# Gated linear and softmax attention on one core: first x chunk transposed on TensorE, value projection by head group, three-bank slots everywhere, new durations in the layout model

## The chip, the cores and the metric

The kernel runs on one core of a Trainium2 chip. The metric is the device time of one execution in microseconds (us), lower is better. Before the change it is 1020.41 us (median of three runs, 1017.95 to 1022.5). TensorE is called PE below, its weight loads PEld, VectorE DVE, ScalarE ACT, GpSimd POOL, and the engine that issues most transfers SP. "The clock" is the granted TensorE clock that the profile shows, as a share of full speed.

## The reference

`x` is 2048 x 512 in bf16, with 32 heads of 16 columns. Branch A is a linear attention with softmax features, branch B an ordinary softmax attention, and a gate mixes them by row.

```python
def _A_ref(x, wqkv, w_phi, wo):
    ...                                            # q, k, v = split(x @ wqkv)
    pq = jnp.einsum("bhsd,hdf->bhsf", q, w_phi)    # the same for k
    phi_q = jnp.concatenate([_softmax(pq), _softmax(-pq)], axis=-1)
    ...
    kv = jnp.einsum("bhsf,bhsd->bhfd", phi_k, v)
    z = jnp.einsum("bhsf->bhf", phi_k)
    num = jnp.einsum("bhqf,bhfd->bhqd", phi_q, kv)
    den = jnp.einsum("bhqf,bhf->bhq", phi_q, z)[..., None] + 1e-6
    return (num / den) ... @ wo

def _B_ref(x, wqkv, wo):
    ...                                            # q, k, v = split(x @ wqkv)
    scores = jnp.einsum("bhqd,bhkd->bhqk", q, k) * (Dh ** -0.5)
    return einsum(softmax(scores), v) ... @ wo

g = _sigmoid((x * gate_w).sum(-1, keepdims=True))
return g * a + (1 - g) * b
```

The heavy part is branch B: 32 heads of 2048 x 2048 scores are 134 million exponentials, and ACT computes every one of them.

## The kernel before

The scores are cut into 2048 tiles of 128 keys x 512 queries. A *slot* is a few tiles next to each other in PSUM: PE computes their scores (QK), ACT takes the exponential of the whole slot in one instruction, PE multiplies with V (PV) and accumulates. Two slots alternate, so ACT can run on one while PE fills the other. A *fill* is any other work for PE (projections, the whole of branch A, the outputs) that is squeezed in between and drained by DVE.

The order of instructions on each engine is not written down. Every operation is registered with an engine, a guessed duration and a priority, and a list scheduler, the *layout model*, plays the program through with those guesses and fixes the order. Each engine is then given its list in that order, with semaphores between the engines. A wrong guess therefore never gives a wrong result, but it can put an instruction in a place where it blocks its engine.

```python
MARGIN = 0.35                       # model: extra delay from DVE/POOL to PE/ACT, and after a DMA
...
op.end = t + op.dur + op.lat        # the scheduler knows nothing but these numbers
...
bS = [Bank(f"S{i}", psS[:, 512 * i:512 * (i + 1)]) for i in range(6)]   # six banks of slots
EARLY = [bM, bS[2], bS[5], bO]      # banks that early fills may use
MISC = [bM, bS[2], bS[5]]           # banks that other fills may use
...
for c in range(QC):                 # x arrives transposed by DMA, 4 chunks of 512 rows
    for t in range(KT):
        dma("sp", 0.01 * (4 * c + t), lambda e, c=c, t=t: e.dma_start_transpose(
            xT[:, t, NQ * c:NQ * (c + 1)], A_x[0, NQ * c:NQ * (c + 1), 128 * t:128 * (t + 1)]),
            [("xT", t, c)], name=f"x{c}_{t}", issue=0.95, lat=2.2)
for i, (nm, o) in enumerate((("wbk", D), ("wbq", 0), ("wbv", 2 * D))):   # 512 KB each
    dma("act", 0.001 * i, lambda e, o=o: e.dma_start(W_B[:, :, o:o + D], wb_v[:, :, o:o + D]),
        [nm], name=nm, lat=3.0 + 1.5 * i)
...
MM = 0.216                          # model: one fill matmul of 512 columns
...
def v_fill(st, prio, banks=None):   # V of 128 tokens for all 32 heads: 4 matmuls of 512 columns
    f, mm = fill(prio, proj([xT[:, t, 128 * st:128 * (st + 1)] for t in range(KT)],
                            [W_B[:, t, 2 * D:3 * D] for t in range(KT)]), ...)
...
n = 2 if s < 64 else min(3, NTILE - s)   # slots: two tiles wide in the first 64 tiles, then three
...
def add_qk(j):
    def fn(e):
        for m, s in enumerate(range(s0, s0 + n)):
            ins = e.matmul(psS[:, 512 * (base + m):512 * (base + m + 1)],
                           lhsT=kT_B[32 * i:32 * i + 32, hg // 2, 128 * kt:128 * (kt + 1)],
                           rhs=qz[32 * i:32 * i + 32, qc % 2, hg, :], ...)
    op = P.add("pe", 0.30, -100, fn, ...)
...
# branch A, normalising one group: PE multiplies phi(q) with kv|z into psM, DVE divides
f, mm = fill(prio + 0.1, mms, [("phiQT", b), "kz0", "kz1"], ..., dur=0.065)
drain(f, mm, "dve", 0.15, -3, ... e.tensor_single_scalar(dr3, ap[...], 1e-6, ALU.add), last=False)
P.add("dve", 0.12, -3, lambda e, dr=dr: e.reciprocal(dr, dr), ...)
P.add("dve", 0.1, -3, lambda e, dr=dr: e.tensor_scalar(dr, dr, g128[:, i:i + 1], None, op0=ALU.mult), ...)
drain(f, mm, "dve", 0.42, -3, fn, ...)       # oA = num * dr, frees psM
```

Because slots are only two tiles wide in the first 64 tiles, banks 2 and 5 of the slots are free for fills there: the first block needs all of V, and that is 16 fills.

The softmax here doesn't subtract the row's maximum and nothing guards it: scores larger than these inputs give would overflow.

Of the kernel before, what the change touches and what calls it, by code (L numbers as in the profile page):

```python
# [6 lines left out]
BF16 = mybir.dt.bfloat16  # L7
# [6 lines left out]
D = 512  # L14
# [12 lines left out]
MARGIN = 0.35  # L27
# [233 lines left out]
def _build(ctx, nc, A_x, A_wqkv, A_w_phi, A_wo, B_wqkv, B_wo, gate_w, out):  # L261
# [34 lines left out]
    fin = sb([128, 2, D], name="fin")  # L296
# [10 lines left out]
    gwb = sb([128, KT, 128], name="gwb")  # L307
# [11 lines left out]
    for b in (0, 1, 3, 4):  # L319
        bS[b].free = False  # L320
    EARLY = [bM, bS[2], bS[5], bO]
    MISC = [bM, bS[2], bS[5]]
# [7 lines left out]
    for c in range(QC):  # L330
        for t in range(KT):
            dma("sp", 0.01 * (4 * c + t), lambda e, c=c, t=t: e.dma_start_transpose(
                xT[:, t, NQ * c:NQ * (c + 1)], A_x[0, NQ * c:NQ * (c + 1), 128 * t:128 * (t + 1)]),
                [("xT", t, c)], name=f"x{c}_{t}", issue=0.95, lat=2.2)
    wb_v = B_wqkv.rearrange("(t p) c -> p t c", p=128)
    wa_v = A_wqkv.rearrange("(t p) c -> p t c", p=128)
    for i, (nm, o) in enumerate((("wbk", D), ("wbq", 0), ("wbv", 2 * D))):
        dma("act", 0.001 * i, lambda e, o=o: e.dma_start(W_B[:, :, o:o + D], wb_v[:, :, o:o + D]),
            [nm], name=nm, lat=3.0 + 1.5 * i)
    for rr in range(8):  # L340
        dma("sp", 1.0 + 0.01 * rr, lambda e, rr=rr: e.dma_start_transpose(
            WAT[:, rr, :], A_wqkv[:, 128 * rr:128 * (rr + 1)]), [("WAT", rr)], name=f"wat{rr}", issue=0.95, lat=2.2)
# [8 lines left out]
    def warm_fn(e):  # L351
        ins = None
        for _ in range(14):
# [6 lines left out]
                                                                    writes=writes, name=name)  # L360
    pool(0.2, -9, lambda e: e.iota(ptmp[:].rearrange("p (a c) -> p a c", c=8), [[-32, 4], [0, 8]],
# [14 lines left out]
    pool(0.3, -7, lambda e: e.iota(ident[:], [[-1, 128]], channel_multiplier=1,  # L376
                                   allow_small_or_imprecise_dtypes=True), writes=["id"], name="id0")
    pool(0.5, -7, lambda e: e.tensor_single_scalar(ident[:], ident[:], 0.0, ALU.is_equal), reads=["id"],
         writes=["ident"], name="ident")
# [24 lines left out]
    MM = 0.216  # L404
# [35 lines left out]
    def k_fill(r, c, prio, banks=None, eng="dve"):  # L440
        f, mm = fill(prio, proj([W_B[:, t, D + 128 * r:D + 128 * (r + 1)] for t in range(KT)],
                                [xT[:, t, NQ * c:NQ * (c + 1)] for t in range(KT)]), ["wbk"] + xk(c), banks,
# [4 lines left out]
    def v_fill(st, prio, banks=None):  # L447
        f, mm = fill(prio, proj([xT[:, t, 128 * st:128 * (st + 1)] for t in range(KT)],
                                [W_B[:, t, 2 * D:3 * D] for t in range(KT)]), ["wbv"] + xk(st // 4), banks,
                     name=f"V{st}")  # L450
        dst = vaug[:, st, 0:H * VW].rearrange("p (h c) -> p h c", c=VW)[:, :, 0:DH]
        drain(f, mm, "dve", 0.69, prio, lambda e, ap: e.tensor_copy(dst, ap.rearrange("p (h d) -> p h d", d=DH)),
              writes=[("v", st)], name=f"Ve{st}")

    def q_fill(r, qc, prio, banks=None, first=False):
        f, mm = fill(prio, proj([W_B[:, t, 128 * r:128 * (r + 1)] for t in range(KT)],
                                [xT[:, t, NQ * qc:NQ * (qc + 1)] for t in range(KT)]), ["wbq"] + xk(qc), banks,
# [14 lines left out]
    while s < NTILE:  # L472
        base = 3 * (len(slots) % 2)
        n = 2 if s < 64 else min(3, NTILE - s)
        slots.append((s, n, base))
        s += n
    NS = len(slots)
    first3 = [j for j, x in enumerate(slots) if x[1] == 3][:2]
# [8 lines left out]
    def add_qk(j):  # L487
# [17 lines left out]
        op = P.add("pe", 0.30, -100, fn, reads=reads, writes=[("S", j % 2)], name=f"qk{j}")  # L505
        if j in first3:
            op.take = [bS[base + 2]]
# [10 lines left out]
    def add_pv(j):  # L518
# [4 lines left out]
        for b, ss in parts.items():  # L523
            def fn(e, ss=ss):
                ins = None
                for s in ss:
# [3 lines left out]
                    ins = e.matmul(psO[32 * i:32 * i + 32, :], lhsT=vaug[:, kt, VW * h:VW * h + 32],  # L530
# [3 lines left out]
            kts = sorted({dec(s)[2] for s in ss})  # L534
            op = P.add("pe", 0.30, -50, fn, reads=[("E", j % ERING), "v1", "v2"] + [("v", k) for k in kts],
# [9 lines left out]
    def add_norm(b, pv):  # L545
# [5 lines left out]
        P.add("dve", 0.15, -40, lambda e: e.reciprocal(rd[:, bb, :], tv[:, :, DH]), reads=[("Tf", bb)],  # L551
              writes=[("rd", bb)], name=f"rd{b}")
        P.add("dve", 0.1, -40, lambda e: e.tensor_tensor(rd[:, bb, :], rd[:, bb, :], gT[:, 2, 16 * qc:16 * qc + 16],
# [3 lines left out]
        P.add("dve", 0.35, -40, lambda e: e.tensor_tensor(  # L557
            tbv, tv[:, :, 0:DH], rd[:, bb, :].unsqueeze(2).to_broadcast([128, 16, DH]), ALU.mult),
            reads=[("Tf", bb), ("rd2", bb), ("rd", bb)], writes=[("TB", par)], name=f"tb{b}")
        if par == 1:  # L560
            P.add("dve", 0.6, -40, lambda e: e.transpose(oT[:, qc % 2, r, :], TB[:]), reads=[("TB", 0), ("TB", 1)],  # L561
# [14 lines left out]
    def put(tile):  # L576
        P.add("sp", 0.1, 0, lambda e: e.dma_start(out[0, 128 * tile:128 * (tile + 1), :], fin[:, tile % 2, :]),
              reads=[("fin", tile % 2)], writes=[("out", tile)], name=f"put{tile}", sem=osem(tile), lat=2.0)
# [10 lines left out]
    def out_tile(qc, i):  # L589
# [3 lines left out]
        drain(f, mm, "dve", 0.69, 0, lambda e, ap: e.tensor_copy(fin[:, tile % 2, :], ap),  # L593
              writes=[("fin", tile % 2)], name=f"Oe{tile}")
# [9 lines left out]
    def out_post(i):  # L604
# [3 lines left out]
        drain(f, mm, "dve", 0.75, 0, lambda e, ap: e.tensor_tensor(fin[:, tile % 2, :], ap, pre[:, i, :], ALU.add),  # L608
              reads=[("pre", i)], writes=[("fin", tile % 2)], name=f"Oe{tile}")
        put(tile)  # L610

    def gate():
        for c in range(QC):
            f, mm = fill(30 + c, proj([gwb[:, t, :] for t in range(KT)],
                                      [xT[:, t, NQ * c:NQ * (c + 1)] for t in range(KT)]),
                         xk(c) + [("gwb", t) for t in range(KT)], name=f"G{c}")
# [17 lines left out]
    wp_ops = []  # L634

# [7 lines left out]

    def va_fill(st, prio):
# [177 lines left out]
```

## Time and profile before

| | before |
|---|---|
| median | 1020.41 us |
| span of the profiled execution | 1015.9 us |
| ACT busy | 958.5 us (94%) |
| ACT idle | 57.4 us |
| first exponential starts | 17.36 us |
| mean granted clock | 0.694 |

Three lines of the page of before: the busy time of the engines (with the share of the span, and the number of instructions), the clock in forty equal slices (in tenths), and who the time belongs to in the chain of waits that ended last.

```profile
PE 864.9 (85%) x5118; PEld 210.8 (21%) x5118; DVE 309.8 (30%) x595; ACT 958.5 (94%) x729; POOL 141.8 (14%) x131
...
PEclk8999999997968868955557655555556655555765
...
ACT 71%; PE 17%; DVE 9%; DMA 1%; issue 1%; SPq 0%; POOL 0%; DVEq 0%
```

ACT bounds the kernel. What is to be gained is its idle time, about 57 us. PE is 85% busy, and the second line says that in most of the second half its clock is near 0.5, so this "85%" is not spare capacity.

The groups of before, kept apart by shape (count | busy us, mean ns of one | idle before, and what ended it). A shape is partitions x elements.

```profile
L512 ACT ACTIVATE E_t<-psS 128x1536 bf16<-128x1536 f32 x661 | 903.8, 1707 | 30.4 <-PE psS L500 24.8 <-PE psO L530 5.3
...
L512 ACT ACTIVATE E_t<-psS 128x1024 bf16<-128x1024 f32 x32 | 30.2, 1030 | 2.6 <-PE psS L500 1.6 <-PE psO L530 0.9
```

The mean is that of one instruction from start to end. Consecutive exponentials overlap, so the busy time divided by the count is the better price: 1.37 us for a slot of three, 0.94 us for a slot of two. Three tiles in slots of two cost 1.41.

PE's waits in before (us in total, times, longest; oA is the last operation with which DVE normalises a group of branch A):

```profile
PE psM L719 <- DVE oA_t L737: 9.9, 14, 1.4
...
PE psM L739 <- DVE oA_t L737: 3.0, 4, 1.5
...
PE psM L712 <- DVE oA_t L737: 2.1, 6, 0.6
```

ACT waits 26.4 us for scores. PE is late with the scores because, among other things, it stands 15 us in front of the one bank psM until DVE has normalised such a group. The second item is another wait: 6.2 us, five times, all between 43 and 61 us. Exponentials are written into a ring of eight buffers, and a buffer is free again only when PE has done the PV that reads it. PE does the last fill of V at 60 us, so PV is late there, and ACT stands before a full ring: the exponential at 51.04 us starts 0.04 us after the PV that frees its buffer, 2.1 us after its scores were ready.

The same execution by stretches. The columns are the stretch, its length, the busy time of PE, PEld, DVE, ACT and POOL (with instructions), the clock, the share of the DMA engines, and GB/s.

```profile
0.00:25.00 25.00, 17.88 (x73) 5.77 (x73) 5.25 (x10) 9.52 (x11) 13.62 (x35) 0.86 0.73 149
25.00:100.00 75.00, 65.89 (x429) 18.90 (x425) 36.15 (x65) 67.80 (x59) 7.32 (x7) 1.00 0.15 35
100.00:225.00 125.00, 105.15 (x808) 33.26 (x808) 89.86 (x141) 125.00 (x99) 65.14 (x49) 1.00 0.00 1
225.00:475.00 250.00, 208.73 (x1385) 62.15 (x1382) 128.50 (x278) 231.51 (x175) 55.71 (x41) 0.75 0.01 3
475.00:950.00 475.00, 416.04 (x2159) 79.77 (x2156) 40.39 (x88) 470.19 (x350) 0.00 (x0) 0.54 0.01 3
```

Length minus ACT's busy time is ACT's idle time: 15.5 us at the head, 7.2 us to 100 us, none to 225 us, 18.5 us in the middle, 4.8 us in the long late stretch, and the rest at the end.

Lines of before's timeline (start us, duration us, engine, line, operation; in brackets the idle time before it and what ended that): the head, one multiply of the middle, and the tail.

```profile
12.30 3.57 PE L435 MATMUL psS<-xT_t,WB_t 128*128 128x512 bf16 x8 [5.75 <-DMA xT_t<-in_A_x_dram]
...
15.91 0.69 ACT L462 ACTIVATE qz_t<-psS,pmask_t 128x512 bf16<-128x512 f32 x1 [9.96 <-PE psS L435]
...
17.36 15.12 ACT L512 ACTIVATE E_t<-psS 128x1024 bf16<-128x1024 f32 x16 [0.77 <-PE psS L500]
...
225.81 1.89 DVE L730 TENSOR_SCALAR denr_t<-denr_t,g_t 128x16 f32<-128x16 f32 x1
...
1012.46 1.29 DVE L608 TENSOR_TENSOR fin_t<-psS,WAT_t 128x512 bf16<-128x512 f32 x2 [1.23 <-DMA out_dram<-fin_t]
```

PE waits 5.75 us for the transposing DMA of x, and the first exponential starts at 17.36 us. At the tail DVE waits 1.23 us for an output transfer to free one of two buffers.

### The profile page before, as it was taken

To read this page: it belongs to the slowest core of one execution; us is meant where nothing else is said; L and a number is where in the kernel's file an instruction comes from. 1 tells how busy PE (TensorE), PEld (TensorE's weight loads), DVE (VectorE), ACT (ScalarE), POOL (GpSimd) and SP (SyncE) were. 2 spreads that over 40 slices of the span, in tenths; PEclk is the share of its full clock that TensorE was granted. 3 is DMA by queue.
4 is the path that set the end of the run, shared out by engine and by line. 5 is a ranking of instruction groups with operands and counts; after the bars stand their busy time and mean duration, and the time that the engine had idled before them with its cause. 6 is when DMAs were issued, how large, how long until landed. Compare 5 with 4: busy or idle time off the path is not lost.

```text
span 1015.9 us, 11834 instructions
## 1 busy us (share of the span) xinstructions
PE 864.9 (85%) x5118; PEld 210.8 (21%) x5118; DVE 309.8 (30%) x595; ACT 958.5 (94%) x729; POOL 141.8 (14%) x131
## 2 busy tenths in 40 slices
PE   7988888878798788788889888888889888888986
PEld 2222222222222232211112111111111111111211
DVE  2346776776744757400002000000001100000101
ACT  3889999998989989999999999999999999999996
POOL 5003554542610603000000000000000000000000
PEclk8999999997968868955557655555556655555765
DMA  7400000000000000000000000000000000000000
GB/s 150 99 2 1 1 1 1 1 1 1 1 7 16 1 1 1 1 1 1 1 1 11 11 1 1 1 0 1 1 1 6 16 1 1 1 1 0 1 1 21
DMA packets 18964, 9.16 MB, mean 9 GB/s; under 512 B 13792, under 2 KB 18912, under 8 KB 18912
## 3 DMA queue, kind: packets, MB, share of 16 engines
q1 hardware_dynamic: 16944, 6.82, 2.8%
q10 hardware_dynamic: 1584, 1.57, 0.6%
q8 instruction: 40, 0.66, 0.3%
q0 software_dynamic: 384, 0.02, 0.0%
q14 instruction: 12, 0.10, 0.0%
HBM read 3.16 MB, written 2.10 MB: 5 GB/s over the span
## 4 chain that ended last, share of the span: by engine, by line
ACT 71%; PE 17%; DVE 9%; DMA 1%; issue 1%; SPq 0%; POOL 0%; DVEq 0%
ACT E_t L512 69%; PE psM L435 6%; PE psS L500 4%; PE psO L530 3%; ACT EA_t L670 2%; PE psS L435 1%; DVE oA_t L737 1%; PE psM L712 1%; DVE denr_t L730 1%; DVE stat_t L674 1%; PE psM L719 1%; DVE Pf_t L655 1%; DMA xT_t<-in_A_x_dram 1%; PE psM L739 1%; DVE denr_t L728 1%
## 5 line engine op out<-in xcount | busy, mean ns | idle before, releaser
L512 ACT ACTIVATE E_t<-psS 128x1536 bf16<-128x1536 f32 (+2 forms) x694 | 934.5, 1675 | 33.0 <-PE psS L500 26.4
L500 PE MATMUL psS<-qz_t,kTB_t 32*128 32x512 bf16 x2048 | 363.5, 521 | 98.8 <-ACT E_t L512 95.4
L530 PE MATMUL psO<-E_t,vaug_t 128*32 128x512 bf16 x2048 | 366.7, 526 | 1.2 <-DVE Tf_t L548 0.8
L500 PEld LDWEIGHTS psS<-qz_t,kTB_t 32*128 32x128 bf16 x2048 | 70.8, 96 | 397.3 <-ACT E_t L512 348.4
L548 DVE STREAM_TRANSPOSE Tf_t<-psO 128x512 f32<-128x512 f32 x32 | 22.8, 713 | 400.7 <-PE psO L530 400.7
L530 PEld LDWEIGHTS psO<-E_t,vaug_t 128*32 128x32 bf16 x2048 | 71.3, 99 | 245.2 <-issue 230.8
L664 POOL TENSOR_TENSOR Dd_t<-Pf_t,stat_t 128x512 bf16<-128x512 f32 x32 | 33.9, 1061 | 185.7 <-DVE stat_t L659 175.3
L464 DVE TENSOR_SCALAR qz_t<-psM,pmask_t 128x512 bf16<-128x512 f32 x30 | 21.9, 729 | 104.0 <-PE psS L500 94.2
L435 PE MATMUL psM<-Wp_t,xT_t 128*128 128x512 bf16 x128 | 38.4, 406 | 4.0 <-DVE phiQT_t L715 1.0
L674 DVE TENSOR_REDUCE stat_t<-EA_t 128x64 f32<-128x1024 bf16 x32 | 38.6, 1207 | 5.2 <-ACT EA_t L670 5.0
L435 PE MATMUL psM<-xT_t,WB_t 128*128 128x512 bf16 x112 | 34.6, 418 | 5.7 <-DVE qz_t L464 2.2
L670 ACT ACTIVATE EA_t<-Dd_t 128x1024 bf16<-128x1024 bf16 x32 | 38.4, 1201 | 0.0
L678 POOL TENSOR_TENSOR phiK_t<-EA_t,stat_t 128x1024 bf16<-128x1024 bf16 x16 | 30.8, 1927 | 36.8 <-DVE stat_t L676 29.6
L667 POOL TENSOR_TENSOR Dd_t<-stat_t,Pf_t 128x512 bf16<-128x512 f32 x32 | 34.2, 1068 | 3.9 <-DVE stat_t L661 2.8
L678 POOL TENSOR_TENSOR phiQ_t<-EA_t,stat_t 128x1024 bf16<-128x1024 bf16 x16 | 30.7, 1927 | 28.4 <-DVE stat_t L676 24.1
L655 DVE COPY Pf_t<-psM 128x512 f32<-128x512 f32 x32 | 22.0, 688 | 28.5 <-PE psM L435 27.3
L593 DVE CAST fin_t<-psM 128x512 bf16<-128x512 f32 x12 | 8.3, 692 | 48.2 <-PE psM L435 48.2
L435 PE MATMUL psM<-WoA_t,phiK_t 128*128 128x512 bf16 x64 | 21.1, 442 | 1.8 <-DVE oA_t L737 0.2
L435 PE MATMUL psM<-WoB_t,oT_t 128*128 128x512 bf16 x61 | 20.3, 416 | 2.5 <-DVE oT_t L561 2.5
L659 DVE TENSOR_REDUCE stat_t<-Pf_t 128x32 f32<-128x512 f32 x32 | 21.7, 679 | 0.9
L661 DVE TENSOR_REDUCE stat_t<-Pf_t 128x32 f32<-128x512 f32 x32 | 21.4, 670 | 0.0
L719 PE MATMUL psM<-kzbd_t,phiQT_t 128*128 128x68 bf16 x128 | 10.9, 216 | 10.9 <-DVE oA_t L737 9.9
(92 smaller groups left out, 340.6 us busy)
## 6 DMA issues: line engine op xcount, KB each, us to landing
out_dram<-fin_t SPq DMA_DIRECT2D x16, 128.0 KB, 1.7
WB_t<-in_B_wqkv_dram ACTq DMA_DIRECT2D x3, 512.0 KB, 5.9
WvA_t<-in_A_wqkv_dram SPq DMA_DIRECT2D x1, 512.0 KB, 4.2
WoA_t<-in_A_wo_dram SPq DMA_DIRECT2D x1, 512.0 KB, 5.1
WoB_t<-in_B_wo_dram SPq DMA_DIRECT2D x1, 512.0 KB, 6.0
xT_t<-in_A_x_dram SPq DMA_TRANSPOSE x16, 4.3
Wbd_t<-in_A_w_phi_dram POOLq DMA_DIRECT2D x8, 2.0 KB, 4.6
WAT_t<-in_A_wqkv_dram SPq DMA_TRANSPOSE x8, 2.8
```

The lines of the kernel that those rows point to most:

```text
L435: return [lambda e, ap, i=i: e.matmul(ap, lhsT=lhs[i], rhs=rhs[i], start=(i == 0), stop=(i == len(lhs) - 1)) for i in range(len(lhs))]
L464: fn = lambda e, ap, dst=dst, par=par: e.tensor_scalar(dst, ap, pmask[:, par:par + 1], None, op0=ALU.mult)
L500: ins = e.matmul(psS[:, 512 * (base + m):512 * (base + m + 1)], lhsT=kT_B[32 * i:32 * i + 32, hg // 2, 128 * kt:128 * (kt + 1)], rhs=qz[32 ...
L512: op = P.add("act", 0.07 + 0.000833 * 512 * n, 0.0, lambda e: e.activation(Ebuf[:, j % ERING, 0:512 * n], psS[:, 512 * base:512 * (base + ...
L530: ins = e.matmul(psO[32 * i:32 * i + 32, :], lhsT=vaug[:, kt, VW * h:VW * h + 32], rhs=Ebuf[:, j % ERING, 512 * m:512 * (m + 1)], start=(k ...
L548: P.add("dve", 0.69, -50, lambda e: e.transpose(Tf[:, bb, :], psO[:]), reads=["psO"], writes=[("Tf", bb)], after=[pv], name=f"T1.{b}")
L655: drain(f, mm, "dve", 0.69, prio, lambda e, ap: e.tensor_copy(Pf[:, b, :], ap), writes=[("Pf", b)], name=f"Pe{qk}.{st}")
L664: P.add("pool", 1.1, prio, lambda e: e.tensor_tensor(dv[:, :, 0:DH], p3, mx.unsqueeze(2).to_broadcast([128, H, DH]), ALU.subtract), reads= ...
L667: P.add("pool", 1.1, prio, lambda e: e.tensor_tensor(dv[:, :, DH:32], mn.unsqueeze(2).to_broadcast([128, H, DH]), p3, ALU.subtract), reads ...
L670: ex = P.add("act", 0.93, -4, lambda e: e.activation(EA[:, b, :], Dd[:, b, :], ACTF.Exp), reads=[("D", b, 0), ("D", b, 1)], writes=[("EA", ...
L674: P.add("dve", 1.22, prio, lambda e: e.tensor_reduce(stat[:, b, 1, :], e3, AX.X, ALU.add), reads=[("EA", b)], writes=[("ss", b)], name=f"s ...
L678: P.add("pool", 2.0, prio, lambda e: e.tensor_tensor(dst.rearrange("p (g f) -> p g f", f=DH), e3, stat[:, b, 1, :].unsqueeze(2).to_broadca ...
```

## The change

The intent: start the exponentials earlier, use three-tile slots from the start, spread V over the blocks that need it so that the first block can live with one spare bank, and let the layout model place instructions by durations that were measured.

- **Head.** Chunk 0 of x comes by plain DMAs and is transposed by 16 matmuls on PE, evicted half by DVE and half by ACT. The weights of branch B come as the 128 columns of the first head group, then the other 384.
- **V by head group.** A fill gives V of 512 tokens for 8 heads: 16 matmuls of 128 columns. The first block then needs 4 such fills, not 16.
- **Three-tile slots everywhere**, and only psM for fills.
- **Durations** of the model and its margins.
- **Tail.** Four output buffers (in the memory of a dead weight) for two.

```diff
-MARGIN = 0.35
+MARGIN = 0.6
-    fin = sb([128, 2, D], name="fin")
+    fin = WvA                                   # four buffers, tile % 4
-    EARLY = [bM, bS[2], bS[5], bO]
-    MISC = [bM, bS[2], bS[5]]
+    FIRST = [bM, bO, bS[3], bS[4], bS[5]]
+    EARLY = [bM, bO]
+    MISC = [bM]
-    for c in range(QC):
+    xs = Dd[:]...
+    for i in range(4):
+        dma("sp", 0.001 * i, lambda e, i=i: e.dma_start(xs[:, i, :], A_x[0, 128 * i:128 * (i + 1), :]), ...)
+    for c in range(1, QC):
         for t in range(KT):
             dma("sp", 0.01 * (4 * c + t), lambda e, c=c, t=t: e.dma_start_transpose(...
-                [("xT", t, c)], name=f"x{c}_{t}", issue=0.95, lat=2.2)
+                [("xT", t, c)], name=f"x{c}_{t}", issue=1.4, lat=2.5)
-    for i, (nm, o) in enumerate((("wbk", D), ("wbq", 0), ("wbv", 2 * D))):
+    for i, (nm, o, n) in enumerate((("wbk0", D, 128), ("wbq0", 0, 128), ("wbv0", 2 * D, 128),
+                                    ("wbk", D + 128, 384), ("wbq", 128, 384), ("wbv", 2 * D + 128, 384))):
         dma("act", 0.001 * i, ...
-    MM = 0.216
+    MM = 0.25
-    def v_fill(st, prio, banks=None):
-        f, mm = fill(prio, proj([xT[:, t, 128 * st:128 * (st + 1)] for t in range(KT)],
-                                [W_B[:, t, 2 * D:3 * D] for t in range(KT)]), ...
+    def v_fill(r, c, prio, banks=None):
+        mms = [lambda e, ap, i=i, t=t: e.matmul(
+            ap[:, 128 * i:128 * (i + 1)], lhsT=xT[:, t, NQ * c + 128 * i:NQ * c + 128 * (i + 1)],
+            rhs=W_B[:, t, 2 * D + 128 * r:2 * D + 128 * (r + 1)], start=(t == 0), stop=(t == KT - 1))
+            for i in range(4) for t in range(KT)]
-        n = 2 if s < 64 else min(3, NTILE - s)
+        n = min(3, NTILE - s)
-        op = P.add("pe", 0.30, -100, fn, ...)   # QK, and PV likewise
+        op = P.add("pe", 0.34, -100, fn, ...)
-        ex = P.add("act", 0.93, -4, ... ACTF.Exp)   # branch A
+        ex = P.add("act", 1.2, -4, ... ACTF.Exp)
-            drain(f, mm, "dve", 0.15, -3, ... 1e-6, ALU.add)        # the normalising group
+            drain(f, mm, "dve", 0.18, -3, ... 1e-6, ALU.add)
-            P.add("dve", 0.12, -3, ... e.reciprocal(dr, dr) ...
+            P.add("dve", 0.25, -3, ... e.reciprocal(dr, dr) ...
-            P.add("dve", 0.1, -3, ... e.tensor_scalar(dr, dr, g128[:, i:i + 1] ...
+            P.add("dve", 0.38, -3, ... e.tensor_scalar(dr, dr, g128[:, i:i + 1] ...
+    for i in range(4):
+        mms = [lambda e, ap, i=i, t=t: e.transpose(..., xs[:, i, 128 * t:128 * (t + 1)], ident[:]) for t in range(KT)]
+        f, mm = fill(-1.0, mms, [("xs", i), "ident"], FIRST, name=f"X{i}", chunk=4, dur=0.08)
+        ...                                     # evicted by ACT if i % 2 else by DVE
     # cut: twelve more durations of DVE, the priorities of the projections, the 17-column PV of
     # the last head of a group, the identity matrix built first, gwb in the memory of EA
```

## The prediction

> **What bounds the kernel now.** ScalarE. The page shows ACT busy 958.5 us of a 1015.9 us span (94%); the chain of waits puts 69% on the softmax exponentials. Groups by form: 661 activations of 128x1536, 903.8 us (1.37 us each), and 32 of 128x1024, 30.2 us (0.94 us each). Gain: 57 us of ACT idle. By windows: 16 us at the head (first exponential at 17.36 us), 8 us from 17 to 100 us, 18 us from 225 to 425 us, 6 to 7 us later, 10 us at the end.
>
> **Head.** The first projection starts at 12.3 us: PE waits 5.8 us for the transposing DMA of x, issued from 0.73 us at 1.25 us apiece; then runs cold (matmuls 0.43 us apart). The change loads x chunk 0 with plain DMAs, transposes it on TensorE and splits the weight loads, so the first group needs 0.9 MB; windows show 300 GB/s from 3 to 7 us. Estimate: data at 6 to 7 us, as warm-up matmuls end (6.54 us); 16 transposes at 0.10 us; four evictions of 0.4 to 0.7 us on two engines; K and Q 0.9 us each if warm; the ACT eviction 0.7 us. First exponential at 12 to 14 us: saves 4.5 us. K of chunk 1 still needs transposing DMAs, now later, and stands before the third slot's QK: may cost 1 us.
>
> **Three-bank slots.** 32 activations of 0.94 us become 21.3 of 1.37: saves 1 us.
>
> **Value projection.** 64 matmuls of 512 columns (0.216 us apart, 14 us) become 256 of 128. [...]128-column transposes cost 13.2/128 = 0.103 us. So about 26 us: +12.6 us of PE where it has room, but three quarters leave the first block. From 17 to 100 us idle falls from 8 to 4 us.
>
> **Layout.** Between 225 and 425 us PE waits 16 us for the DVE group that normalises the linear branch (0.17+0.24+0.38+0.42 us and gaps, modelled as 0.79). ACT starves, and the granted clock alternates between 0.5 and 1.0. [...] New durations remove most of these waits. But in instruction order the linear branch ends 52 slots later and thinner (0.3 to 0.46 us of fill per slot, before 0.45 to 0.5), so cold spells stay. Estimate: idle from 18 to 13 us.
>
> **Tail.** DVE waits 1.2 us for an output DMA to free one of two buffers; four end that: 1 us.
>
> **Sum.** 4.5 + 1 + 4 - 1 + 5 + 1, about 15 us: **1005 us**, range 994 to 1016. Faster by over 2%: 0.25; within 2%: 0.73; slower: 0.02.
>
> **Right if:** first exponential before 14 us; exponentials 933 us in sum, all but the last 1536 wide; ACT's waits for QK fall from 26 to 18 us; PE's waits for the normalising group nearly vanish; no wait before the last additions.
>
> **Wrong if:** x or weights land after 8 us, so PE goes cold again; the single PSUM bank left to projections starves ACT early; or the thinner linear branch holds PE at half clock, so that each fill stalls ACT and the middle gains nothing (1012 us). If the middle idles only 10 us: 993 us.

4.5 + 1 + 4 - 1 + 5 + 1 comes to 14.5, the "about 15 us". "Cold" and "half clock" can be read in the trace of before: the clock is 0.50 from about 9.0 to 15.8 us, PE having stood still from 6.5 to 12.3; it is 0.50 from 435 to 545 us, where PE has little but scores and PV (88% busy), and 1.00 from 550 to 560 us, where output projections run between them (97% busy). That a thinner linear branch means cold spells was the estimate; these stretches fit it.

## More of the kernel before

The two items of ACT's waits before exponentials in before (us in total, times, longest):

```profile
ACT E_t L512 <- PE psS L500: 26.4, 45, 1.7
...
ACT E_t L512 <- PE psO L530: 6.2, 5, 2.0
```

## The result, and the profile after

The result is correct. The time is 994.33 us (median of four, 992.58 to 998.74), against 1021.26 us for before in the same rounds. The ratio is 0.9748, with a 95% interval of 0.9705 to 0.979. A ratio here is always the mean time of one kernel's fast runs over that of the other's in the same rounds, so it is not quite the ratio of the medians quoted.

| | before | after |
|---|---|---|
| median, same rounds | 1021.26 | 994.33 |
| profiled span | 1015.9 | 991.0 |
| ACT busy / idle | 958.5 / 57.4 | 955.4 / 35.6 |
| first exponential | 17.36 | 11.54 |
| mean granted clock | 0.694 | 0.725 |

The page of after, the same three lines:

```profile
PE 832.2 (84%) x5280; PEld 219.6 (22%) x5326; DVE 312.6 (32%) x597; ACT 955.4 (96%) x720; POOL 141.7 (14%) x131
...
PEclk9999999998697957789858555555556755555775
...
ACT 83%; PE 10%; DVE 5%; DMA 1%; issue 1%; POOL 1%; another core or an unknown queue 0%; ACTq 0%; DVEq 0%; POOLq 0%
```

ACT's share of the chain rises from 71% to 83%, and PE's falls from 17% to 10%: there are fewer detours.

Groups of after by shape:

```profile
L522 ACT ACTIVATE E_t<-psS 128x1536 bf16<-128x1536 f32 x682 | 936.4, 1766 | 19.1 <-PE psS L510 18.2
...
L456 PE MATMUL psM<-WB_t,xT_t 128*128 128x128 bf16 x256 | 20.5, 224 | 1.0 <-DVE kTB_t L451 0.6
```

The longest item of ACT's waits in after:

```profile
ACT E_t L522 <- PE psS L510: 18.2, 26, 2.0
```

PE's waits in after:

```profile
PE psM L734 <- DVE oA_t L752: 4.2, 8, 1.6
...
PE psM L442 <- DVE oA_t L752: 2.4, 3, 1.3
...
PE psM L727 <- DVE oA_t L752: 1.8, 6, 0.6
```

ACT's wait for scores went from 26.4 to 18.2 us. PE's three largest waits for the normalising group went from 15.0 to 8.4 us, so they nearly halved, and did not vanish (with the smaller ones, 16.2 and 9.7 us). The wait for PV is gone. The 256 matmuls of V are 20.5 us of busy time, 0.080 us each.

After by stretches, columns as above:

```profile
0.00:25.00 25.00, 19.95 (x141) 8.74 (x142) 5.91 (x12) 13.71 (x12) 13.65 (x35) 0.93 0.90 159
25.00:100.00 75.00, 63.93 (x491) 21.42 (x496) 35.44 (x63) 75.00 (x59) 11.60 (x9) 1.00 0.12 33
100.00:225.00 125.00, 102.92 (x824) 35.95 (x835) 71.72 (x111) 125.00 (x98) 47.59 (x37) 1.00 0.00 1
225.00:475.00 250.00, 205.15 (x1482) 66.43 (x1498) 149.62 (x310) 236.17 (x180) 68.88 (x51) 0.80 0.01 3
475.00:950.00 475.00, 410.92 (x2205) 81.50 (x2212) 43.62 (x90) 473.04 (x352) 0.00 (x0) 0.58 0.01 3
```

From 25 to 225 us ACT is not idle for a moment. The middle is still the largest loss with 13.8 us.

Now the sum can be made. The stages do not end at the same microsecond in the two kernels, so the late stretch is taken from 475 us to 41 us before the end.

| where the 24.9 us of the span came from | us |
|---|---|
| ACT idle, 0 to 25 us (15.5 to 11.3) | 4.2 |
| ACT idle, 25 to 100 us (7.2 to 0) | 7.2 |
| ACT idle, 225 to 475 us (18.5 to 13.8) | 4.7 |
| ACT idle, 475 us to 41 us before the end (6.5 to 2.0) | 4.5 |
| ACT idle, last 41 us (9.8 to 8.6) | 1.2 |
| ACT busy (958.5 to 955.4) | 3.1 |

Lines of after's timeline: the head, one passage of the middle, and the tail.

```profile
11.54 2.79 ACT L522 ACTIVATE E_t<-psS 128x1536 bf16<-128x1536 f32 x2 [0.49 <-PE psS L510]
...
15.03 0.81 PE L442 MATMUL psO<-xT_t,WB_t 128*128 128x512 bf16 x3 [2.99 <-POOL mask_t L405]
...
16.21 1.45 ACT L522 ACTIVATE E_t<-psS 128x1536 bf16<-128x1536 f32 x1 [1.87 <-PE psS L510]
...
265.36 1.93 POOL L693 TENSOR_TENSOR phiQ_t<-EA_t,stat_t 128x1024 bf16<-128x1024 bf16 x1 [6.66 <-DVE stat_t L691]
265.43 1.89 DVE L745 TENSOR_SCALAR denr_t<-denr_t,g_t 128x16 f32<-128x16 f32 x1
...
267.36 0.42 DVE L752 TENSOR_TENSOR oA_t<-psM,denr_t 128x256 bf16<-128x256 f32 x1
...
267.84 0.41 PE L734 MATMUL psM<-kzbd_t,phiQT_t 128*128 128x68 bf16 x4 [1.63 <-DVE oA_t L752]
...
268.83 1.45 ACT L522 ACTIVATE E_t<-psS 128x1536 bf16<-128x1536 f32 x1 [1.42 <-PE psS L510]
...
986.89 1.88 DVE L619 TENSOR_TENSOR WvA_t<-psS,WAT_t 128x512 bf16<-128x512 f32 x3
```

Three things are to be read here. First, the head: the exponentials start 5.8 us earlier, but after two of them ACT stops. The next score needs K of chunk 1, which PE can start only at 15.03 us, after 3.0 us of waiting. The releaser that the profile prints (a mask on POOL) has nothing to do with K; the transposing DMA of chunk 1 is the other suspect, and is tested below. Second, the middle: a DVE multiply of 128 x 16 numbers, started 0.07 us after a POOL multiply, takes 1.89 us and ends when POOL's ends; then oA, then PE, then ACT are late in turn, and ACT loses 1.42 us. Third, the tail: the last three additions run without a gap, where before waited 1.23 us.

The tile view says how odd that multiply is (ns minimum/median/maximum of 32, then first and last start):

```profile
L743 DVE RECIPROCAL denr_t<-denr_t x32: 195/253/253, 255.0 to 461.4; 128x16 f32<-128x16 f32 x32
L745 DVE TENSOR_SCALAR denr_t<-denr_t,g_t x32: 134/234/1891, 255.6 to 461.7; 128x16 f32<-128x16 f32 x32
L752 DVE TENSOR_TENSOR oA_t<-psM,denr_t x32: 365/425/426, 256.2 to 461.9; 128x256 bf16<-128x256 f32 x32
```

Its neighbours, on the same data, never take longer than 0.43 us. Of the 32 multiplies, six are above 0.3 us in after (0.34, 1.89, 0.95, 1.26, 1.89 and 0.55), and four in before (1.89, 1.48, 1.54 and 0.50). Each of these ten ends 0.03 us after a POOL instruction that was running when it started. The new "measured duration" of 0.38 us in the layout model is the mean of two modes: most take 0.23, a few far more, and hardly any 0.38.

### The profile page after: what moved, and what is told of

The parts are those of the page before. It is cut to its first block, busy times and chain, and to the rows that moved or that the text cites. A ratio compares the mean times of both kernels' runs of the same rounds, so it can differ in the third digit from the quotient of the medians.

```text
span 991.0 us, 12194 instructions
## 1 busy us (share of the span) xinstructions
PE 832.2 (84%) x5280; PEld 219.6 (22%) x5326; DVE 312.6 (32%) x597; ACT 955.4 (96%) x720; POOL 141.7 (14%) x131
## 4 chain that ended last, share of the span: by engine, by line
ACT 83%; PE 10%; DVE 5%; DMA 1%; issue 1%; POOL 1%; another core or an unknown queue 0%; ACTq 0%; DVEq 0%; POOLq 0%
ACT E_t L522 81%; PE psS L510 3%; PE psO L541 3%; PE psM L442 2%; ACT EA_t L685 2%; PE psM L727 1%; DMA gw_t<-in_gate_w_dram 1%; DVE denr_t L745 1%; DVE stat_t L689 1%; DVE qz_t L475 1%; PE psM L734 1%; DVE Pf_t L670 0%; DVE oA_t L752 0%; DVE stat_t L674 0%; PE psM L754 0%
## 5 line engine op out<-in xcount | busy, mean ns | idle before, releaser
L522 ACT ACTIVATE E_t<-psS 128x1536 bf16<-128x1536 f32 (+1 forms) x683 | 937.3, 1765 | 19.1 <-PE psS L510 18.2
L510 PE MATMUL psS<-qz_t,kTB_t 32*128 32x512 bf16 x2048 | 348.3, 504 | 110.0 <-ACT E_t L522 103.7
L541 PE MATMUL psO<-E_t,vaug_t 128*32 128x512 bf16 (+1 forms) x2048 | 356.9, 509 | 0.7 <-ACT E_t L522 0.5
L541 PEld LDWEIGHTS psO<-E_t,vaug_t 128*32 128x32 bf16 (+1 forms) x2048 | 70.6, 97 | 233.6 <-issue 221.5
L685 ACT ACTIVATE EA_t<-Dd_t 128x1024 bf16<-128x1024 bf16 x32 | 45.2, 1413 | 0.0
L604 DVE CAST WvA_t<-psM 128x512 bf16<-128x512 f32 x12 | 8.3, 691 | 48.9 <-PE psM L442 48.9
L674 DVE TENSOR_REDUCE stat_t<-Pf_t 128x32 f32<-128x512 f32 x32 | 21.8, 681 | 1.0
L456 PE MATMUL psM<-WB_t,xT_t 128*128 128x128 bf16 x256 | 20.5, 224 | 1.0 <-DVE kTB_t L451 0.6
L463 DVE CAST vaug_t<-psM 128x512 bf16<-128x512 f32 x16 | 11.1, 693 | 25.9 <-PE psM L456 25.9
```

What stands on the lines that cost most here:

```text
L522: op = P.add("act", 0.07 + 0.000833 * 512 * n, 0.0, lambda e: e.activation(Ebuf[:, j % ERING, 0:512 * n], psS[:, 512 * base:512 * (base + ...
L541: ins = e.matmul(psO[32 * i:32 * i + w, :], lhsT=vaug[:, kt, VW * h:VW * h + w], rhs=Ebuf[:, j % ERING, 512 * m:512 * (m + 1)], start=(kt ...
L685: ex = P.add("act", 1.2, -4, lambda e: e.activation(EA[:, b, :], Dd[:, b, :], ACTF.Exp), reads=[("D", b, 0), ("D", b, 1)], writes=[("EA", ...
```

## The experiments

The prediction's total was 15 us, the measurement 27. The questions were: which part of the change earns what; whether the middle is held by a cold clock, as the prediction said, or by something else; and whether the head's late chunk is real. Four kernels take one part back each (head_old, dur_old, v_whole and two_bank; dur_new_only is the reverse of dur_old), then dur_new_only, warm_full, warm_qk and rest_late test the durations, the middle and the head, then four the explanations that were left. Times are medians, and before was run in the same rounds each time (1019 to 1021 us). ACT's idle time is given by the stretches of the tables above, always of one profiled execution. No run takes back the other parts of the change, such as the 17-column PV or the priorities of the projections: in what follows they belong to the new structure.

| kernel | median us | range, runs | ratio to before, 95% | ACT idle 0-25, 25-100, 100-225, 225-475, 475-950 |
|---|---|---|---|---|
| before | 1021.26 | 1017.95-1022.5, 4 | 1 | 15.5, 7.2, 0, 18.5, 4.8 |
| after | 994.33 | 992.58-998.74, 4 | 0.9748 (0.9705-0.979) | 11.3, 0, 0, 13.8, 2.0 |
| head_old | 1000.63 | 997.62-1005.99, 6 | 0.9827 (0.9799-0.9854) | 16.2, 1.0, 0.2, 14.2, 1.9 |
| dur_old | 1026.12 | 1024.41-1032.0, 6 | 1.0089 (1.0062-1.0116) | 18.0, 2.2, 0.6, 28.4, 3.3 |
| two_bank | 1012.56 | 995.86-1018.58, 6 | 0.983 (0.978-0.988), two runs | 13.0, 9.3, 1.7, 11.6, 3.9 |
| v_whole | 1018.23 | 1013.45-1020.66, 6 | 0.999 (0.9968-1.0012) | 13.7, 14.8, 2.8, 16.4, 2.6 |
| dur_new_only | 1015.43 | 1012.82-1018.02, 4 | 0.996 (0.9924-0.9996) | 15.6, 9.3, 3.4, 15.3, 3.3 |
| warm_full | 994.01 | 993.04-998.11, 4 | 0.976 (0.9721-0.9799) | 12.9, 0, 0, 11.2, 3.9 |
| warm_qk | 998.79 | 997.36-1001.91, 4 | 0.9801 (0.977-0.9832) | 12.4, 0, 0.4, 17.5, 4.6 |
| rest_late | 992.51 | 989.38-994.38, 4 | 0.9732 (0.9701-0.9763) | 8.4, 0, 0, 17.0, 1.9 |
| pe_old | 1006.97 | 1003.6-1009.06, 4 | 0.9865 (0.9842-0.9887) | 12.5, 3.4, 0.9, 13.2, 4.5 |
| gate_fold | 990.55 | 988.75-994.85, 5 | 0.9713 (0.969-0.9736) | 13.8, 0, 0, 9.0, 2.7 |
| fin_two | 996.35 | 994.25-1003.64, 6 | 0.9781 (0.9749-0.9812) | 13.0, 0, 0.4, 14.0, 1.6 |
| best | 988.74 | 983.32-990.44, 5 | 0.9692 (0.9671-0.9712) | 8.0, 2.4, 0.9, 3.8, 4.8 |

All gave a correct result. Two expectations missed widely: dur_old was put at 8 to 10 us above after and came out 32 above, v_whole at 3 to 6 and came out 24 above. Read the idle columns with care: of the kernels that are meant to differ from after nowhere beyond 475 us (head_old, warm_full, warm_qk, rest_late, gate_fold, best), one reads 1.9 us there and another 4.8, and rest_late, which changes only the order of some loads, reads 17.0 in the middle against after's 13.8. A difference of 3 us in one stretch of one profile proves little by itself.

### head_old: the old head on the new kernel

```diff
-    for i in range(4):                       # plain DMAs of chunk 0, and its 16 transposes: removed
-    for c in range(1, QC):
+    for c in range(QC):
-    ("wbk0", D, 128), ("wbq0", 0, 128), ("wbv0", 2 * D, 128), ("wbk", D + 128, 384), ...
+    ("wbk", D), ("wbq", 0), ("wbv", 2 * D)
```

> The changed kernel with its head undone: x chunk 0 by transposing DMAs, weights in three whole loads, no transposes on TensorE; all else as changed. Theory (the parts add up, each in its own stretch): first exponential at about 17.5 us instead of 11.5, but the 2.8 us of ACT idle between 13 and 20 us, put down to chunk 1 of x landing late, go away; ACT idle in the first 25 us 14 to 15.5 us instead of 11.3; from 25 to 100 us it stays under 1 us; time about 3.5 us above the changed kernel, 998 us. Rival (the early start gives the first block the slack that makes 25 to 100 us quiet): idle of 3 us or more comes back from 25 to 100 us, time 1001 us or more.

Measured: 1000.63 us, 6.3 us more than after. The head idles 16.2 us again, as in before, plus 1.0 us to 100 us; the middle is as in after. So the new head is worth 5 to 6 us (5.2 by the spans of the two profiles, 6.3 by the medians), more than the 3.5 us (4.5 less 1) that the prediction gave it, and it hardly acts on the rest.

### dur_old: the old durations on the new structure

```diff
-MARGIN = 0.6
+MARGIN = 0.35
-    issue=1.4, lat=2.5     # transposing DMAs
+    issue=0.95, lat=2.2
-    MM = 0.25
+    MM = 0.216
-    P.add("pe", 0.34, ...  # QK and PV
+    P.add("pe", 0.30, ...
     # and every duration of DVE and ACT back to its old value
```

> The changed kernel with the old durations and the old margin in the layout model; all else as changed. Theory (the durations cured the late half only): ACT idle from 225 to 475 us back from 13.8 to about 18 us, after 475 us from 2 to about 6 us, 25 to 100 us still under 2 us; time 8 to 10 us above the changed kernel, about 1003 us. Rival (the durations made nearly all of the gain in the middle): 25 to 100 us also idles 5 us or more, time 1008 us or more. Second rival (durations do little; PE idle and clock decide): within 3 us of the changed kernel.

Measured: 1026.12 us, 32 us slower than after and 0.9% slower than before. A line of ACT's waits in dur_old, for the first query projection:

```profile
ACT qz_t L473 <- PE psS L442: 11.4, 1, 11.4
```

There are two losses. The model believed that a transposing DMA lands after 2.2 us, so it put K of chunk 1 in front of the first query projection; PE waits for the DMA (to 15.23 us in its timeline), and ACT waits 11.4 us with it. The new head is then slower than the old one. In the middle the idle time is 28.4 us, and PE's waits for the normalising group are 16 us there, against 8.4 us in after. The old order did fit the old structure better than it fits the new one.

### dur_new_only: the new durations on the old structure

The edit is the reverse: before, with every duration and margin of after.

> The kernel before with nothing but the new durations and margin of the layout model: instruction order changes, no instruction does. Theory (durations act on the middle and the late half, whatever the structure): ACT idle from 225 to 475 us falls from 19 to about 14 us, after 475 us from 6 to 2 us, while 25 to 100 us keeps its 7 us and the head its 15 us; time 8 to 12 us below before, ratio 0.989. Rival (durations matter only where one PSUM bank is left, as in the changed kernel): ratio 0.995 to 1.005.

Measured: 1015.43 us, a ratio of 0.996. The middle gains 3.2 us, but 25 to 225 us loses 5.5 us, so the idle time mostly moves. The parts are not additive. Durations alone give about 4 us, the structure alone costs 9 us, and both together save 26 us.

### v_whole: the V projection by token tile in the new kernel

```diff
-    def v_fill(r, c, ...):   # 16 matmuls of 128 columns, one head group; 4 fills in the first block
+    def v_fill(st, ...):     # 4 matmuls of 512 columns, all heads; 16 fills in the first block
```

> The changed kernel with the value projection by whole rows of tokens again, 64 matmuls of 512 columns, all due in the first block; three-bank slots and the rest as changed. Theory (V by head group spreads PE work out of an overfull first block): PE fill in the first 32 slots is the largest of all, ACT idles 4 to 6 us more before 60 us; later stretches as changed; time 3 to 6 us above the changed kernel. Rival (12.6 us more PE work is a cost that the split pays later): ACT idle from 225 to 475 us falls by 3 us or more and the time is equal or lower.

Measured: 1018.23 us, a ratio of 0.999: without the split of V the whole change is worth nothing. (V's fills also have other priorities here than in before, and K of chunk 1 comes in front of the first scores; the head idles 2.4 us more than in after.) Lines of v_whole's timeline:

```profile
35.02 0.82 PE L442 MATMUL psM<-WB_t,xT_t 128*128 128x512 bf16 x3 [0.79 <-DVE vaug_t L459]
...
37.28 0.82 PE L442 MATMUL psM<-xT_t,WB_t 128*128 128x512 bf16 x3 [0.79 <-DVE vaug_t L459]
...
40.73 8.16 ACT L518 ACTIVATE E_t<-psS 128x1536 bf16<-128x1536 f32 x6 [10.42 <-PE psS L506]
```

The middle line is K of chunk 2, the third chunk (its operands are printed in the other order than those of V). It stands in the queue behind the eight V fills of chunks 0 and 1, the last of which take turns in the one bank psM: each of these waits 0.79 us until DVE has emptied the bank. ACT runs out of scores for 10.4 us in a row. Three-tile slots and V by head group are one package: wide slots take the two spare banks away, and only fewer fills in the first block make that bearable.

### two_bank: two-tile slots in the first block of the new kernel

```diff
-        n = min(3, NTILE - s)
+        n = 2 if s < 64 else min(3, NTILE - s)
-    MISC = [bM]
+    MISC = [bM, bS[2], bS[5]]        # EARLY and FIRST likewise
```

> The changed kernel with two-bank slots in the first 64 tiles and three PSUM banks for projections there, as before the change; all else as changed. Theory (the wide slot itself is worth 1 to 1.5 us of fixed cost, and V by head group cured the rest): time 1 to 2 us above the changed kernel, ACT idle from 25 to 100 us under 1.5 us. Rival (two-tile slots overload PE, which is what made ACT idle there): idle of 4 us or more from 25 to 100 us, time 5 us or more above.

Measured: six runs from 995.86 to 1018.58 us, so this kernel has two modes. Only the fastest two (995.86 us at a clock of 0.735, 1007.10 us at 0.709) count as fast, and the ratio rests on those two. The four slower ones, the profiled one among them, show a mean clock of 0.702 to 0.709, and one fast run has that clock too. One line of the profiled run by stretches:

```profile
36.00:50.00 14.00, 14.00 (x63) 3.78 (x63) 1.53 (x3) 9.88 (x10) 0.00 (x0) 0.50 0.16 53
```

The stretches on both sides read the same: from 22 to 56 us PE is busy all the time at a clock of 0.50, and ACT is busy only 25.5 of those 34 us. Since the profiled run is a slow one, I do not use it for a difference between two_bank and after; what it does show is that PE can read as fully busy for 34 us without its clock rising. Whether wide slots are worth more than the prediction's 1 us therefore stays open: the fastest two-tile run equals after, the other five are slower by 13 to 24 us.

### warm_full and warm_qk: is the middle held by a cold clock?

The prediction's theory was that the thin linear branch leaves PE at half clock, so that each fill stalls ACT. The rival was that PE waits in its queue for DVE whatever the clock. Both kernels give PE useless work in the slots of the middle, to raise the clock.

```diff
+            if 450 <= s0 < 960:       # warm_full: one full-array matmul before the scores, overwritten by them
+                e.matmul(psS[:, 512 * base:512 * (base + 1)], lhsT=kT_B[:, hg // 2, ...], rhs=qz[:, qc % 2, hg, :], ...)
```

```diff
-            for m, s in enumerate(range(s0, s0 + n)):       # warm_qk: the scores computed twice
+            again = 2 if 450 <= s0 < 960 else 1
+            for m, s in [x for _ in range(again) for x in enumerate(range(s0, s0 + n))]:
```

> The changed kernel, and ahead of each QK group from tile 450 to 960 one more matmul over the whole 128x128 array, 512 columns, into the same bank, which the QK then overwrites: results as before, 0.22 us more PE work per slot. Theory (what is left of ACT idle in the middle comes from PE falling to half clock when fills are thin): granted clock 0.95 or more from 230 to 475 us, ACT idle there from 13.8 to under 5 us, time 8 to 10 us below the changed kernel. Rival (order and waits on VectorE make the idle, or PE has no room): idle equal or larger, time 5 us or more above.

> The changed kernel with each QK group from tile 450 to 960 issued twice into the same banks (results as before): each matmul fills 32 of 128 rows of the array, three at a time, some 0.3 us more PE work per slot at full clock and 0.5 at half. Theory A (the clock follows PE busy time): as with the whole-array matmul, clock 0.95 or more and ACT idle under 5 us. Theory B (the clock follows how much of the array works): the clock stays at or below that of the changed kernel, about 0.8, PE is overfull at half clock and ACT idles 20 us or more in that stretch, time 10 us or more above the changed kernel.

Measured: 994.01 and 998.79 us. The middle of warm_full:

```profile
225.00:475.00 250.00, 219.44 (x1669) 74.24 (x1669) 151.86 (x313) 238.81 (x182) 70.01 (x52) 0.97 0.01 3
```

The clock is at 0.97 instead of 0.80, and ACT's idle time 11.2 instead of 13.8 us; the total time does not move. Neither side of the expectation came true: the theory wanted idle time under 5 us, the rival a time 5 us higher. In warm_qk the clock is 0.92 and the idle time 17.5 us (in the slowest of its four runs), but that kernel also issues each set of scores twice (a set of three takes 0.39 us in after at a clock of 1.00, and 0.61 at 0.50), so warm_full is the cleaner of the two. It isn't free either: PE has 14 us more work in this stretch (219.4 us against 205.2), in front of the scores. So what is shown is that a warm clock bought with such work gains no time; what a warm clock at no cost would gain was not tested. PE's waits for the normalising group stay, 9.0 us against 9.7 in after, and they are the next suspect. In gate_fold and best, below, the clock of this stretch is 0.85 and 0.89 without any warming, so part of the half clock may be a result of the waits and not their cause. What sets the clock no run here settles: warm_qk, which adds only matmuls on 32 rows, reached 0.92 over the middle, and yet stayed at 0.50 from 228 to 240 us with PE busy for 11.2 of the 12 us.

### pe_old: only PE's three durations back

```diff
-    MM = 0.25
+    MM = 0.216
-    P.add("pe", 0.34, ...  # QK and PV
+    P.add("pe", 0.30, ...
```

> The changed kernel with only three numbers of the layout model put back, those for TensorE: 0.216 instead of 0.25 us for a 512-column matmul, 0.30 instead of 0.34 us for a QK or PV group. Theory (of the 32 us that all old durations cost, the middle part came from TensorE taken for faster than it is, so fills are packed ahead of QK; the head part of 7 us from the DMA numbers): ACT idle from 225 to 475 us back to 22 us or more from 13.8, head unchanged, time 10 to 20 us above the changed kernel. Rival (VectorE durations of the normalising group did it, as predicted): time within 4 us of the changed kernel.

Measured: 1006.97 us, 12.6 us slower than after, but not where it was looked for. The middle idles 13.2 us, the same as after; the loss is 3.4 us from 25 to 100 us, 0.9 us to 225 us, 2.5 us late, 1.2 us at the head and 3.3 us of ACT's busy time (broken runs of exponentials: the first after a gap shows 1.45 us, one in a run 1.34). Both sides of the expectation missed. My reading, argued and not tested, is that a model that takes PE for 12 to 14% faster than the new durations do crowds fills into slots that have no room, in the stretches where PE is fullest. The 15 us that the middle loses in dur_old (28.4 against 13.2) belong to the durations that pe_old leaves new (DVE, ACT, the margins and the DMAs), alone or together with PE's. That agrees with the predicted mechanism, the better placed normalising group, but the four are not separated.

### rest_late: the head's late chunk

```diff
-        dma("act", 0.001 * i, ...                # six weight loads: 3 x 128 KB, then 3 x 384 KB
+        dma("act" if i < 3 else "sp", 0.001 * i if i < 3 else 0.5 + 0.001 * i, ...
```

This puts the 1.1 MB that nobody needs yet behind all transposing DMAs of x.

> The changed kernel with the three 384 KB weight loads of later head groups moved behind the transposing loads of x, on the sync queue. Theory (they delay x chunk 1, which is what K of chunk 1, and the third QK behind it, waits for until 15.0 us): chunk 1 is used by 12.5 us, ACT idle after the first exponential in the first 25 us falls from 2.8 us to under 0.7 us, time 2 to 3 us below the changed kernel. Rival (transposing DMAs are slow by themselves, 1.3 us of issue each and 4 to 6 us to land): chunk 1 still comes after 14.5 us, time within 1 us.

Measured: 992.51 us, against 994.33; the intervals overlap, so the total alone proves nothing. The timeline of rest_late's head does:

```profile
11.40 14.88 ACT L523 ACTIVATE E_t<-psS 128x1536 bf16<-128x1536 f32 x11 [0.49 <-PE psS L511]
11.75 1.04 PE L443 MATMUL psO<-xT_t,WB_t 128*128 128x512 bf16 x4
```

K of chunk 1 runs at 11.75 instead of 15.03 us, without a wait, and eleven exponentials follow each other without a gap. The median time from issue to landing of the transposing DMAs of x falls from 5.9 to 4.0 us. So the releaser that after's profile printed was wrong, and the cause was the DMA: the transposes land later while weights that are not urgent are in flight (the DMA engines are 90% busy in after's first 25 us). The head gains 2.9 us of ACT's time; the total gains less, and this profile has 17.0 us of idle time in the middle; whether that is spread or an effect of the edit is open.

### gate_fold: the slow multiply removed

The rival for the middle, by then, was that multiply. Its gate factor can go into the operation that reads PSUM: the denominator is multiplied by 1/gate = 1 + exp(-z), which the kernel holds already, and the reciprocal then gives gate/denominator.

```diff
-    e.tensor_single_scalar(dr3, ap[...][:, :, 64:68], 1e-6, ALU.add)
+    e.tensor_scalar(dr3, ap[...][:, :, 64:68], 1e-6, g128[:, i:i + 1], op0=ALU.add, op1=ALU.mult)   # g128 = 1/gate
     e.reciprocal(dr, dr)
-    P.add("dve", 0.38, -3, lambda e, dr=dr: e.tensor_scalar(dr, dr, g128[:, i:i + 1], None, op0=ALU.mult), ...)
```

> The changed kernel without the 32 VectorE multiplications of the reciprocal denominator by the gate (0.23 us at best, 1.6 to 1.9 us when a GpSimd multiplication runs): the denominator is multiplied by 1/gate in the instruction that reads it from PSUM, which gives the same after the reciprocal. Theory (that instruction waits for GpSimd, VectorE then holds the one PSUM bank, TensorE waits, ACT starves): ACT idle from 225 to 475 us from 13.8 to 6 to 9 us, waits of TensorE for the normalising group from about 10 to under 4 us, time 4 to 8 us below the changed kernel. Rival (these waits fall where there is slack): within 2 us.

Measured: 990.55 us. The middle:

```profile
225.00:475.00 250.00, 208.32 (x1537) 66.86 (x1537) 145.07 (x285) 241.05 (x184) 70.11 (x53) 0.85 0.01 3
```

ACT idles 9.0 us instead of 13.8, PE's waits for the group fall to 6.5 us (from 9.7, all of them counted), and none of the group's remaining operations takes longer than 0.43 us. Both fall short of what the theory expected (waits under 4 us, a time 4 to 8 us lower). The expectation's 1.6 to 1.9 us is the long end only: with POOL running, the slow multiplies of after took 0.34 to 1.89 us. The same read with the factor folded in is 0.23 us at the median instead of 0.18. Two effects are in this number: the stalls go (in after they add up to 5.5 us over the normal 0.23), and each of the 32 groups is one operation shorter. The run does not split them. For the middle there is more than one profile to compare: after, head_old, fin_two and rest_late, which keep the multiply and are not meant to change the middle, idle 13.8, 14.2, 14.0 and 17.0 us there; gate_fold and best, which do not, 9.0 and 3.8. The total is 3.8 us below after's, and the intervals of the two ratios overlap (0.969 to 0.9736 against 0.9705 to 0.979), so it is the traces that carry this more than the total.

### fin_two: two output buffers again

```diff
-    fin = WvA
+    fin = sb([128, 2, D], name="fin")        # tile % 2
```

> The changed kernel with two output buffers of their own again in place of four in the former value weights. Theory (VectorE stands still for output DMAs at the tail and at each of the three earlier output stages): 1.2 us back at the tail and 0.5 to 1 us of ACT idle at each stage near 290, 530 and 760 us, time 2 to 4 us above the changed kernel. Rival (only the tail notices): 1 to 1.5 us above, the late-half idle of ACT stays at 2 us and its fall from 6 us is the durations' doing.

Measured: 996.35 us, 2.0 us above after, with overlapping intervals. In the trace the wait of 1.23 us for the output DMA before the last additions is back, as long as in before. The late stretch idles 1.6 us, so the buffers are not what made the late half better: they matter in the last microseconds alone.

### best: rest_late and gate_fold together

> The changed kernel with the late weight loads moved behind x and the gate folded into the denominator, both at once. If the two add up: head idle 8.3 us instead of 11.3, idle from 225 to 475 us 6 to 9 us, time 983 to 988 us, ratio to before 0.964 to 0.970. If the head's gain is given back later, or the fold does nothing, 990 us or more.

Measured: 988.74 us (983.32 to 990.44), a ratio of 0.9692. The ratio is inside the expected range and the median 0.7 us above it. In the profiled run, the fastest of the five, the head idles 8.0 us and the middle 3.8 us:

```profile
225.00:475.00 250.00, 203.70 (x1566) 65.99 (x1566) 141.97 (x282) 246.23 (x189) 68.75 (x51) 0.89 0.01 3
```

It has the lowest time; its interval ends at 0.9712, so it lies clear of before and of most kernels here, but touches those of gate_fold (from 0.969), rest_late (from 0.9701) and after (from 0.9705). Between 25 and 225 us it gives 3.2 us back, and 2.8 us late.

## Why the prediction was right or wrong

The direction was right, and the range (994 to 1016) held 994.33 by 0.33 us, with two of the four runs below 994: that is luck, for the sum behind it was 1005. The size was not right: 15 us were predicted, 27 measured, and the more likely outcome, within 2%, is not what happened.

- **What bounds the kernel.** Right: ACT, and its idle time. Of the 24.9 us of the span, 21.8 are idle time that went.
- **First exponential before 14 us.** Right, with 11.54 us; the step was undersized, 4.5 us predicted and 5.8 measured. "K of chunk 1 ... may cost 1 us" was the right place and too small: the gaps that follow are 1.87, 0.39 and 0.53 us in after, 2.8 us together, and rest_late shows their cause.
- **Exponentials 933 us, all but the last 1536 wide.** Right within 0.5%: 936.4 us for 682 and one last, narrower, 937.3 in all. But before's sum was 934.5, so the saving of 1 us does not show in it. ACT's busy time as a whole fell by 3.1 us, and fewer gaps can account for it: an exponential after a gap costs 0.1 us more of busy time than one in a run, and ACT's busy time in the profiles rises with the number of its gaps, from 953.2 us at 24 gaps over 0.1 us (best) through 955.4 at 33 (after) and 958.5 at 54 (before) to 960.5 at 67 (dur_old).
- **"From 17 to 100 us idle falls from 8 to 4 us."** Wrong in size, and the largest mis-sized term that is clear of the spread: from 25 to 100 us it fell by 7.2 us to zero. The place was right (the first block is relieved of V), but the idle time was nearly all one wait, ACT before a full ring because PV is late, and it went as a whole. The cost of V was sized from transposes at 0.103 us, and the 256 matmuls cost 0.080 us each (20.5 us, not 26). The 0.103 was a mean of two clocks: of before's 128 transposes, 68 ran at the full clock and took 0.079 us each, 60 at half and took 0.131; V runs almost wholly at the full clock (1.00 from 25 to 225 us in after). The 0.080 us are busy time and not the spacing: in the timeline of after, runs of 4, 8 and 12 of V's matmuls take 0.40, 0.62 and 0.84 us, so one follows the other by 0.055 us, and the rest is the start and end of each short run. On weight loads, the trace of before shows 0.099 us on average for 128 columns (0.096 to 0.138 by group) and 0.099 for 32. More important, v_whole shows that the split is not a cost with a small gain elsewhere: it is what makes the one-bank first block work at all.
- **Three-tile slots: 1 us.** Not settled by itself. two_bank ran between 996 and 1019 us.
- **Layout: idle from 18 to 13 us in the middle.** The number was right (18.5 to 13.8), as was that of ACT's waits for scores over the whole run (26.4 to 18.2 us, 18 predicted); the reasoning only by half. The waits for the normalising group were to "nearly vanish", and only nearly halved (15.0 to 8.4 us). "Cold spells stay" was true of the clock (0.80), but nothing shows it to be the cause: at 0.97 the time is the same (warm_full, with 14 us more PE work). What keeps a good part of the rest is a DVE multiply that stands still until a POOL instruction ends; it reads its tensor and a scalar per row from SBUF. That it stands still, the trace shows: 1.89 us instead of 0.23, ending 0.03 us after POOL's 1.93 us, while the operations around it, with at most one tensor or scalar per row from SBUF, are never slow (0.43 us at most). Why it stands still, no run here shows. Two multiplies of branch B that read two tensors from SBUF are stretched in the same way, in after up to 1.14 us (median 0.175) and 1.31 us (median 0.424); gate_fold leaves them in. gate_fold, which takes the multiply of the denominator away, lowers the idle time further than the warm kernels do (9.0 us against 11.2 and 17.5), and best has 3.8 us left. The trace of before held the stalls as well (1.89, 1.48 and 1.54 us), so they do not explain the difference between before and after; they explain part of what remained. I had read the mean of 0.38 us and not the spread.
- **Late half: nothing.** The profiles read 4.5 us (6.5 to 2.0), and no gain was predicted there. How much of it is real is open: kernels with after's late half read 1.9 to 4.8 us, so up to 2.8 us of the 4.5 can be the spread of single profiles. dur_old and dur_new_only each read 3.3 us from 475 to 950 us, between before's 4.8 and after's 2.0. fin_two excludes the output buffers. Which other part of the change did it, if any, stays open too.
- **Tail: 1 us, no wait before the last additions.** Right: 1.2 us.
- **The sum was built of independent parts.** That is the step behind the others. The runs show that they are not independent: durations alone 0.4%, structure alone a loss of 0.9%, both together a gain of 2.5%. An order made by a model is tuned to its structure, and each part taken alone lands in somebody else's schedule.

By terms, in us saved:

| term of the sum | predicted | measured |
|---|---|---|
| head, with the late chunk | 3.5 | 4.2 in idle; 6.3 by head_old |
| 17 (25) to 100 us | 4 | 7.2 |
| middle | 5 | 4.7 |
| late half | 0 | 4.5 (1.7 to 4.5 by the spread) |
| tail | 1 | 1.2 |
| ACT busy | 1 | 3.1 |

## What to carry to other kernels

When a scheduler with guessed durations fixes the order, correct the durations and the structure together and measure them together, since each alone can lose; and look at the spread of every duration you feed it, because a mean of 0.38 us can be 0.23 us with an occasional stall of 1.9. Before you blame a cold PE clock for waits, raise the clock with useless work in that stretch (here from 0.80 to 0.97, with 14 us of it), and count what that work costs: if the time stays, look at who holds the buffer. Loads that nobody needs yet belong behind the transposing DMAs of the first data, even when their own queue is free: those landed after 4.0 us here instead of 5.9.
